# A GpSimd queue in which each product waits for the end of the one before, and value pooling moved to VectorE

## The chip, the core and the metric

The kernel runs on one core of a Trainium2 chip. It uses the core's engines side by side, each with a queue of its own: TensorE (PE; its weight loads are shown apart as PEld), VectorE (DVE), ScalarE (ACT), GpSimd (POOL) and SyncE (SP), which issues the transfers from and to HBM. Engines wait for each other by semaphores. The metric is the time of one execution on the device in microseconds; the median of several runs counts.

## The reference

Three blocks follow one another, all in float32, on 4 batches x 576 positions = 2304 rows of width 512 (8 heads of 64).

```python
# attention; q, k, v are [4, 8, 576, 64]
q_d, k_d, v_d = (x.reshape(B, H, 144, 4, 64).mean(axis=3) for x in (q, k, v))
out_d = sm_attn(q_d, k_d, v_d)                  # attention over 144 pooled positions
out_up = np.repeat(out_d, 4, axis=2)
mask = np.abs(pos[:, None] - pos[None, :]) < 4  # local attention: 3 keys to either side
scores = np.where(mask, scale * q @ k.T, -1e9)
out_local = softmax(scores) @ v
x = out_up + out_local                          # then heads joined: [2304, 512]
# block 1: h = x @ w_in [512, 2048]
g = np.maximum(h, 0) + alpha * np.minimum(h, 0)
x = g @ w_out                                   # [2048, 512]
# block 2
xn = x / np.sqrt(np.mean(x * x, -1, keepdims=True) + 1e-6) * rms_g
g, val = xn @ w_gate, xn @ w_val                # [512, 1536] each
out = (g * sigmoid(g) * val) @ w_out2           # [1536, 512]
```

## The kernel before

**Matmuls.** Each float32 operand is split in two half-precision parts (`split` at L435 to L437: ACT writes the high part, L436, DVE the low part, L437), and a product is three matmuls. Block 1 works on blocks of 384 columns (two groups of 192): `h_mm` (matmuls at L1429, ACT's relu at L1433, DVE's correction at L1435, then `split`) makes the hidden layer, `o_mm` (L1446) the output. Block 2 works on pairs of such blocks with fewer, larger products (`pair_f`, L1681).

**Attention.** Batch 0 and the first group of batch 1 use matmuls for the local attention too (`Dense`). The other eight groups, 4 to 11, use `local_tasks`: 128 partitions hold 32 stretches of rows x 4 pairs of heads, 6 rows each. For two rows and one head of the pair at a time, one POOL operation multiplies q by its seven neighbouring keys (L542; the product has 2 x 7 x 64 = 896 elements per partition and is named `prod`), and DVE sums over the 64 (L553). After the softmax (POOL at L566 to L584, small), one POOL operation multiplies the seven weights by the values (L596, `prod` again), and DVE sums over the seven (L609). That is 6 products of either kind per group, 48 and 48 in all, through two `prod` buffers.

**Pooling.** `down_tasks` does the pooled attention of batches 1 to 3, one pair of heads at a time (4 per batch). For each of q, k and v it loads a tile `sd` (72 partitions x 2 x 2 x 256), ACT squares v for a bound on its size (L691), and `pool` sums four rows to one by two additions: in place into `sd` (L705, 512 elements), then into `qkp` for q and k or `dd` for v (L707, 256 elements). In batch 1 DVE does them, in batches 2 and 3 POOL. The next head's load of v goes into the buffer that these sums read.

**Weights.** Between the other work, weights are decoded from int32 halves (L1183, L1186 on ACT, L1188 on DVE, 768 elements, two inputs in SBUF) and split.

**The order.** All instructions are traced first; `issue_order` (L76) then plays the program through with a cost for each instruction (`cost`), lags between engines, and a port that DVE and POOL share in its model, and orders each engine's queue by the due times that come out. A table `LEADS` shifts the due times of ranges of instructions, in ns, before the last pass. The order is then written down as dependencies between neighbours in a queue, without any semaphore wait:

```python
    info = mybir.DependencyInfo(mybir.DependencyClass.NoSync, mybir.DependencyReason.DATA)
    for q in best[1].values():
        for a, b in zip(q, q[1:]):
            tc.add_manual_dep(insts[b], insts[a].name, info, reason="issue order")
```

So a POOL instruction waits by semaphore only for what it needs: its inputs, and its buffer. Each engine takes its queue strictly in this order.

Of the kernel before, what the change touches and what calls it, by code (L numbers as in the profile page):

```python
# [18 lines left out]
def view(ap, dims, off=0, parts=None):  # L19
# [2 lines left out]


LEADS = (
# [48 lines left out]
)  # L73


def issue_order(tc, nc, groups, rounds=40):  # L76
# [3 lines left out]
    count = range(len(insts))  # L80
# [21 lines left out]
    def psum(a):  # L102
        return "PSUM" in str(a.tensor.space)
# [34 lines left out]
    def cost(k, ins, outs):  # L138
        i, e = insts[k], eng[k]
        if not outs:  # L140
            return 60.0
        o, n = outs[0], free(outs[0])
        if e == "SP":
            return transfer(o, ins[0])[0]
        if e == "PE":
            if wide(ins[0]) == 2:
                return max(25.0, n / 2.4 + 2.5)
            return n * 2 / 2.4 + 3 if i.is_transpose else n * 4 / 2.4 + (128 if n < 64 else 8)
        n = max([n] + [free(a) for a in ins[:1]])
        extra = len([a for a in ins[1:] if free(a) == 1 and n > 1])  # L150
        if e == "Activation":
            return (61 if psum(ins[0]) else 103) + n / 1.2 + 93 * (extra + len(outs) - 1)
        if e == "DVE":
            if i.opcode == "Reciprocal":
                return 89 + 6.25 * n
            fast = i.opcode in ("TensorScalarPtr", "TensorCopy") and not any(psum(a) for a in ins)
            fast = fast and len([a for a in ins if free(a) > 1]) < 2
            return 89 + n / (1.92 if fast else 0.96) + 60 * (extra > 0)
        if n <= 4 and ins:
            return 1200.0  # L160
        if i.opcode == "TensorTensor":
            return 148 + 100 * (list(o.ap)[-1][0] == 7) + n * (1.667 if any(list(a.ap)[-1][0] == 0 for a in ins) else 2.104)
        return 36 + 0.83 * n if i.opcode == "Memset" else 370 + 6 * n if i.opcode == "ISA" else 200 + 2.0 * n

    aps = [tuple([a.bass_ap for a in l if hasattr(a, "bass_ap")] for l in (i.ins, i.outs)) for i in insts]
# [4 lines left out]
    def second(k, ins):  # L170
# [5 lines left out]
        if n > 1:  # L176
            return True
        return insts[k].opcode in ("TensorScalarPtr", "TensorCopy") and not any(psum(a) for a in aps[k][0] + aps[k][1])

    shared = [second(k, aps[k][0]) for k in count]  # L180
    users = {}
# [19 lines left out]
    for k, (ins, outs) in enumerate(aps):  # L201
        for l, wr in ((ins, False), (outs, True)):
            for a in l:
                n = a.tensor.name
# [55 lines left out]
    def run(P, S, prio, fwd, d):  # L260
# [9 lines left out]
        for _ in count:  # L270
# [11 lines left out]
                real[k] += max(0.0, port - t)  # L282
                port = t + real[k]
            end[k] = t + real[k]
            clock[e] = end[k] if held[k] is None else t + held[k]
            seq[e].append(k)
            for s in S[k]:
                left[s] -= 1
# [18 lines left out]
            lead[k] += by  # L307
    end, seq, d = run(preds, succs, lead, True, dur)
    best = max(end), seq, lead
    info = mybir.DependencyInfo(mybir.DependencyClass.NoSync, mybir.DependencyReason.DATA)  # L310
    for q in best[1].values():
        for a, b in zip(q, q[1:]):
            tc.add_manual_dep(insts[b], insts[a].name, info, reason="issue order")


@with_exitstack
def kernel(
# [14 lines left out]
    nc = tc.nc  # L332
# [339 lines left out]
    def down_tasks(b, h, tags=(None, None, None), solo=False, dd=("prod", "prod")):  # L672
# [21 lines left out]
        def pool(nm):  # L694
            def f():
# [5 lines left out]
                        st["qkp"] = pool_of(tq).tile([SH, 2, 2, 2, D], F32, tag=tq, name="qkp")  # L701
                    p = st["qkp"][:, 0 if nm == "q" else 1]
                t = t.rearrange("p a j r -> p (a j) r")
                eng = nc.gpsimd if b > 1 and nm in "qkv" else nc.vector
                eng.tensor_tensor(out=t[:, :, 0:2 * D], in0=t[:, :, 0:2 * D], in1=t[:, :, 2 * D:4 * D],  # L705
                                        op=ALU.add)
                eng.tensor_tensor(out=p.rearrange("p a j d -> p (a j) d"), in0=t[:, :, 0:D],  # L707
# [1421 lines left out]
```

## Time and profile before

| | us |
|---|---|
| median of 3 runs | 921.95 |
| lowest, highest | 921.83, 924.78 |
| the profiled execution | 923.82 |
| its span, first to last instruction | 922.1 |
| PE busy | 884.4 |
| DVE busy | 722.5 |
| ACT busy | 567.5 |
| POOL busy | 408.6 |

The profile is of one execution. Its own time is 1.72 us longer than the span that the trace covers, and 1.87 us above the median. Busy times overlap, since the engines work side by side: the one to look at is the engine whose gaps the others fill or make.

### The profile page before, as it was taken

The numbers are of one execution on the slowest core, as the hardware profiler recorded it, in microseconds if no ns is written. First come the engines' busy times: TensorE is split into PE (matmuls) and PEld (weight loads), VectorE is DVE, ScalarE is ACT, GpSimd is POOL, SyncE is SP. The second block draws the span as 40 slices with busy tenths as digits, with TensorE's granted clock in tenths as the row PEclk, the third lists the DMA queues.
The fourth block names the chain that finished last, engine by engine and source line by source line (L and its number), as shares of the span: only waits on it lengthen the run. The fifth ranks groups of instructions, "written<-read, shape, count | busy, mean of one in ns | idle before, by whom it ended". The sixth has DMA issues, their size and how long they took to land.

```text
span 922.1 us, 16731 instructions
## 1 busy us (share of the span) xinstructions
PE 884.4 (96%) x6394; PEld 591.0 (64%) x6394; DVE 722.5 (78%) x1342; ACT 567.5 (62%) x1332; POOL 408.6 (44%) x330
## 2 busy tenths in 40 slices
PE   6977999999999999899999999999999999999997
PEld 5766877689856666566666666654466654566686
DVE  4789987798756887897889898999888883177872
ACT  4999985443674347774598688984266742256730
POOL 1100105887999899687310344211415100077730
PEclk9997999999999999999999999999999999999999
DMA  9976351263423104440152102220100001100001
GB/s 218 296 277 201 93 177 40 61 202 109 122 75 110 48 26 102 140 133 1 36 168 72 36 1 70 86 87 24 35 12 1 1 1 36 33 1 1 1 18 52
DMA packets 54110, 73.80 MB, mean 80 GB/s; under 512 B 22202, under 2 KB 35918, under 8 KB 54030
## 3 DMA queue, kind: packets, MB, share of 16 engines
q1 hardware_dynamic: 54030, 72.74, 27.0%
q8 instruction: 50, 0.82, 0.4%
q14 instruction: 30, 0.25, 0.1%
HBM read 68.01 MB, written 4.72 MB: 79 GB/s over the span
## 4 chain that ended last, share of the span: by engine, by line
PE 76%; DVE 8%; ACT 6%; POOL 3%; issue 3%; DMA 3%; SPq 1%; DVEq 0%; POOLq 0%; ACTq 0%
PE hps L1429 16%; PE acc L1446 15%; PE pa L1681 14%; PE oacc L1804 10%; PE pf L1681 7%; PE pb L1681 3%; PE px L1924 3%; PE py L1924 1%; PE lsps L953 1%; POOL prod L542 1%; DVE xt L437 1%; POOL prod L596 1%; DMA sd<-in_v_dram 1%; DVE ls L553 1%; ACT wr L1183 1%
## 5 line engine op out<-in xcount | busy, mean ns | idle before, releaser
L1429 PE MATMUL hps<-xt,wi 128*128 128x192 f16 (+1 forms) x1536 | 328.7, 290 | 13.9 <-DVE g L437 8.9
L1446 PE MATMUL acc<-ghl,wo 128*128 128x384 f16 (+1 forms) x960 | 228.2, 311 | 2.2 <-ACT ghl L436 2.2
L1429 PEld LDWEIGHTS <-wi 128*128 128x128 f16 x1536 | 150.2, 101 | 61.4 <-issue 10.0
L1446 PEld LDWEIGHTS <-wo 128*128 128x128 f16 x1344 | 128.9, 98 | 64.3 <-issue 9.0
L1681 PEld LDWEIGHTS <-ws 128*128 128x128 f16 x864 | 84.9, 99 | 57.1 <-issue 1.5
L542 POOL TENSOR_TENSOR prod<-cq,ckv 128x896 f32<-128x896 f32 x48 | 101.8, 2135 | 36.2 <-PE tps L1064 28.2
L1804 PE MATMUL oacc<-wi,wo 128*128 128x512 f16 x360 | 99.4, 379 | 0.0
L1681 PEld LDWEIGHTS <-w 128*128 128x128 f16 x648 | 63.8, 99 | 41.9 <-issue 0.6
L1433 ACT ACTIVATE g<-hps 128x384 f32<-128x384 f32 x96 | 47.0, 489 | 68.5 <-PE hps L1429 68.1
L1435 DVE SCALAR_TENSOR_TENSOR hps<-g,oma,hps 128x192 f32<-128x192 f32 (+1 forms) x128 | 66.2, 518 | 28.1 <-ACT g L1433 27.5
L596 POOL TENSOR_TENSOR prod<-ls,ckv 128x896 f32<-128x896 f32 x48 | 86.2, 1847 | 3.5 <-DVE lo L609 2.8
L1446 PE MATMUL acc<-g,wo 128*128 128x384 f16 (+1 forms) x384 | 73.0, 286 | 0.1
L1681 PE MATMUL pb<-x,w 128*128 128x384 f16 x216 | 67.7, 326 | 0.0
L1681 PE MATMUL pa<-x,w 128*128 128x384 f16 x216 | 66.3, 326 | 0.0
L1661 POOL TENSOR_TENSOR ws<-w 128x768 f32<-128x768 f16 x12 | 22.7, 1899 | 97.4 <-DVE ws L1568 41.5
L1804 PEld LDWEIGHTS <-wo 128*128 128x128 f16 x360 | 35.2, 98 | 40.1
L1689 DVE TENSOR_TENSOR sn<-pf,sn 128x384 f32<-128x384 f32 x45 | 24.9, 553 | 43.7 <-PE pf L1681 38.8
L436 ACT ACTIVATE ghl<-hps,grp 128x384 f16<-128x384 f32 (+1 forms) x73 | 42.0, 576 | 26.2 <-DVE hps L1435 15.8
L1686 ACT ACTIVATE sn<-pa 128x384 f32<-128x384 f32 x66 | 31.7, 486 | 42.6 <-PE pa L1681 42.1
L609 DVE TENSOR_REDUCE lo<-prod 128x128 f32<-128x896 f32 x48 | 51.8, 1079 | 7.7 <-POOL prod L596 7.5
L1873 POOL TENSOR_TENSOR wr<-wi 128x512 f32<-128x512 f16 x12 | 15.7, 1305 | 87.7 <-DMA out_dram<-ob 79.6
L553 DVE TENSOR_REDUCE ls<-prod 128x14 f32<-128x896 f32 x48 | 51.7, 1079 | 2.8 <-POOL prod L542 2.7
(366 smaller groups left out, 2117.9 us busy)
## 6 DMA issues: line engine op xcount, KB each, us to landing
wr<-in_moe_w_out_dram SPq DMA_DIRECT2D x18, 512.0 KB
wr<-in_moe_w_in_dram SPq DMA_DIRECT2D x10, 768.0 KB
wr<-in_moe_w_gate_dram SPq DMA_DIRECT2D x8, 768.0 KB
wr<-in_moe_w_val_dram SPq DMA_DIRECT2D x8, 768.0 KB
ckv<-in_k_dram SPq DMA_DIRECT2D x7, 768.0 KB
ckv<-in_v_dram SPq DMA_DIRECT2D x7, 768.0 KB
wr<-in_moe_w_out_dram SPq DMA_DIRECT2D x20, 256.0 KB
out_dram<-ob SPq DMA_DIRECT2D x14, 256.0 KB
```

Source lines behind the costliest of these rows:

```text
L436: nc.scalar.activation(out=hi, in_=src, func=AF.Copy, scale=s)
L542: engs[i].tensor_tensor(out=pr, in0=view(st["q"][:, j, t:t + TP], [[D, TP], [0, ND], [1, D]]), in1=view(st["k"][:, j, t:t + TP], [[D, TP], ...
L553: nc.vector.tensor_reduce(out=st["s"][:, j, t:t + TP], in_=st.pop(("p", i)), axis=AX.X, op=ALU.add)
L596: engs[i].tensor_tensor(out=over(pr, i), in0=view(st["s"][:, j, t:t + TP], [[ND, TP], [1, ND], [0, D]]), in1=view(st["v"][:, j, t:t + TP], ...
L609: nc.vector.tensor_reduce(out=st["o"][:, t:t + TP, j], in_=view(pr, [[ND * D, TP], [ND, D], [1, ND]]), axis=AX.X, op=ALU.add)
L1429: nc.tensor.matmul(ps[:, j], wi[:, f + j, a, kk * 128:(kk + 1) * 128], x[:, b_, kk, c0:c0 + n], start=(i == 0), stop=(i == 3 * KK - 1))
L1433: nc.scalar.activation(out=g, in_=ps, func=AF.Relu, scale=-1.0)
L1435: nc.vector.scalar_tensor_tensor(out=ps[:, j], in0=g[:, j], scalar=oma[:, f + j:f + j + 1], in1=ps[:, j], op0=ALU.mult, op1=ALU.add)
L1446: nc.tensor.matmul(acc[e], wo_f(f)[:, a, e * 128:(e + 1) * 128], hl[:, b_], start=(f == f0 and i == 0), stop=(f == f1 and i == 2))
L1681: nc.tensor.matmul(ps, w[:, a, kk, c:c + 128], x[:, b_, kk], start=(start and n == 0), stop=(n == 3 * K2 - 1), skip_group_check=True)
L1804: nc.tensor.matmul(acc, uhl(f)[:, h, a, tt * 128:(tt + 1) * 128], w[:, b_, f % 3], start=(f == fs[0] and i == 0), stop=(f == fs[-1] and i ...
L1924: nc.tensor.matmul(ps, two(u[g])[:, a, tt * 128:(tt + 1) * 128], w(g, b_), start=(start and g == 0 and i == 0), stop=(g == F2 - 1 and i == 2),
```

## The change

Four things change. (1) In the order written down at the end, the POOL instruction behind one that writes `prod`, `sd`, `qkp` or `dd` now gets a dependency with a semaphore wait: it starts only when that one has ended. The model of `issue_order` puts 120 ns between the two. (2) In batches 2 and 3, `pool("v")` runs on DVE; q and k stay on POOL. (3) The model's costs change for POOL's two-input operations (without a repeated operand 124 + 2.203 n ns instead of 148 + 2.104 n; the 100 ns for a stride of 7 no longer apply to the products with v, whose weights are repeated) and for DVE operations that write with a stride of 8 (65 + 1.8 n; the additions at L645). (4) `LEADS` is another table. No instruction is added or dropped, and no transfer.

```diff
@@ LEADS = (
-    (8123, 8158, -2000), (927, 928, 1000), (8102, 8103, 7000), (8208, 8396, -1500), (2202, 2286, 4000),
...
-    (6529, 6694, 2500), (696, 697, -22500), (8777, 8780, 1500), (6999, 7000, -8000),
+    (8102, 8103, 7000), (776, 777, -500), (3486, 3544, 1500), (7335, 7386, 500), (5591, 5593, -500),
...
+    (6319, 6321, 14500),
 )
@@ def cost(k, ins, outs):
                 return 89 + 6.25 * n
+            if list(o.ap)[-1][0] == 8:
+                return 65 + 1.8 * n
...
         if i.opcode == "TensorTensor":
-            return 148 + 100 * (list(o.ap)[-1][0] == 7) + n * (1.667 if any(list(a.ap)[-1][0] == 0 for a in ins) else 2.104)
+            if any(list(a.ap)[-1][0] == 0 for a in ins):
+                return 148 + n * 1.667
+            return 124 + 100 * (list(o.ap)[-1][0] == 7) + n * 2.203
@@ def issue_order
+    apart = [120.0 if eng[k] == "Pool" and aps[k][1] and
+             aps[k][1][0].tensor.name.split("_")[0] in ("prod", "sd", "qkp", "dd") else 0.0 for k in count]
...
-            clock[e] = end[k] if held[k] is None else t + held[k]
+            clock[e] = end[k] + apart[k] if held[k] is None else t + held[k]
...
-    info = mybir.DependencyInfo(mybir.DependencyClass.NoSync, mybir.DependencyReason.DATA)
+    info, wait = [mybir.DependencyInfo(c, mybir.DependencyReason.DATA)
+                  for c in (mybir.DependencyClass.NoSync, mybir.DependencyClass.Sync)]
     for q in best[1].values():
         for a, b in zip(q, q[1:]):
-            tc.add_manual_dep(insts[b], insts[a].name, info, reason="issue order")
+            tc.add_manual_dep(insts[b], insts[a].name, wait if apart[a] else info, reason="issue order")
@@ def down_tasks, pool(nm)
-                eng = nc.gpsimd if b > 1 and nm in "qkv" else nc.vector
+                eng = nc.gpsimd if nm in {2: "qk", 3: "qk"}.get(b, "") else nc.vector
```

## Rows read from the trace of the kernel before

**Rows 1.** The page: busy time of PE, and shares of the last chain

```profile
PE 884.4 (96%) x6394; PEld 591.0 (64%) x6394; DVE 722.5 (78%) x1342; ACT 567.5 (62%) x1332; POOL 408.6 (44%) x330
...
PE 76%; DVE 8%; ACT 6%; POOL 3%; issue 3%; DMA 3%; SPq 1%; DVEq 0%; POOLq 0%; ACTq 0%
```

**Rows 2.** PE's waits, 147 to 435 us: total, times, longest

```profile
PE hps L1429 <- DVE g L437: 2.4, 3, 1.8
PE acc L1446 <- ACT ghl L436: 2.2, 1, 2.2
PE atps L758 <- ACT dd L749: 2.0, 2, 1.5
PE ltps L997 <- POOL dls L983: 1.5, 1, 1.5
PE hps L1429 <- DVE ghl L437: 1.3, 1, 1.3
PE hps L1429 <- DVE xt L437: 1.2, 1, 1.2
```

**Rows 3.** Stretches: length, busy of PE, PEld, DVE, ACT, POOL; clock, DMA

```profile
240.00:280.00 40.00, 37.76 (x314) 26.52 (x312) 24.91 (x42) 25.05 (x83) 36.58 (x30) 0.96 0.36 102
260.00:380.00 120.00, 120.00 (x819) 75.72 (x818) 91.59 (x148) 62.91 (x184) 109.08 (x79) 1.00 0.28 81
```

**Rows 4.** Timeline of DVE: start, duration, operation, idle time before

```profile
177.78 2.73 DVE L979 TENSOR_SCALAR dlsum<-dlsum 96x8 f32<-96x8 f32 x1 [0.61 <-ACT dls L973]
...
190.82 4.02 DVE L437 SCALAR_TENSOR_TENSOR xt<-dls,sc,xt 128x192 f16<-128x192 f32 x1
...
203.12 0.40 DVE L437 SCALAR_TENSOR_TENSOR xt<-dls,sc,xt 128x192 f16<-128x192 f32 x1
...
374.82 3.93 DVE L1188 SCALAR_TENSOR_TENSOR wc<-wr 128x768 int32<-128x768 int32 x1 [1.02 <-ACT wr L1186]
...
382.94 2.67 DVE L1188 SCALAR_TENSOR_TENSOR wc<-wr 128x768 int32<-128x768 int32 x1 [0.27 <-ACT wr L1186]
...
388.96 0.96 DVE L1188 SCALAR_TENSOR_TENSOR wc<-wr 128x768 int32<-128x768 int32 x1
...
395.25 2.42 DVE L1188 SCALAR_TENSOR_TENSOR wc<-wr 128x768 int32<-128x768 int32 x1
...
848.93 1.36 DVE L1867 SCALAR_TENSOR_TENSOR w<-th,w 128x384 f16<-128x384 f32 x1
```

**Rows 5.** Timeline of POOL, same columns

```profile
177.42 1.29 POOL L705 TENSOR_TENSOR sd<-sd 72x512 f32<-72x512 f32 x1
178.65 1.84 POOL L596 TENSOR_TENSOR prod<-ls,ckv 128x896 f32<-128x896 f32 x1
...
189.03 2.13 POOL L542 TENSOR_TENSOR prod<-cq,ckv 128x896 f32<-128x896 f32 x1
...
193.90 0.72 POOL L707 TENSOR_TENSOR qkp<-sd 72x256 f32<-72x256 f32 x1
...
211.98 5.22 POOL L596 TENSOR_TENSOR prod<-ls,ckv 128x896 f32<-128x896 f32 x3
...
373.02 2.14 POOL L542 TENSOR_TENSOR prod<-cq,ckv 128x896 f32<-128x896 f32 x1
...
414.06 10.54 POOL L542 TENSOR_TENSOR prod<-cq,ckv 128x896 f32<-128x896 f32 x5
...
848.64 1.24 POOL L1893 TENSOR_TENSOR wo<-th,wo 128x384 f32<-128x384 f32 x1
849.96 1.21 POOL L1895 TENSOR_TENSOR sn<-th,wo 128x384 f32<-128x384 f32 x1
```

**Rows 6.** Groups of DVE by shape: first pooling sum, batch 1

```profile
L705 DVE TENSOR_TENSOR sd<-sd 72x512 f32<-72x512 f32 x12 | 8.2, 680 | 2.3 <-DMA sd<-in_q_dram 1.8 <-DMA sd<-in_k_dram 0.5
```

**Rows 7.** The chain that ended last, near 245 us: start, duration

```profile
243.04 0.79 POOL dd L707
...
245.09 8.75 DMA sd<-in_v_dram
```

87 rows, old and new, of the table LEADS are left out of this document.

## The prediction

> **What bounds the kernel now.** I read the page first: TensorE (PE) is busy for 884.4 of 922.1 us, and the chain that ended last runs over PE for 76%, over VectorE (DVE) for 8%, over GpSimd (POOL) for 3% [rows 1]. So PE's own work sets the time, and a change off PE can only give or take PE's gaps: 922.1 - 884.4 = 37.7 us in all. Next I asked who PE waits for in the stretch in which POOL computes the attention products, 147 to 435 us [rows 2]. The reader is to see six kinds of wait, 2.4 + 2.2 + 2.0 + 1.5 + 1.3 + 1.2 = 10.6 us; most name DVE, or an engine that itself stood behind DVE. Then the table by stretch [rows 3]: from 260 to 380 us PE has no gap (120.00 of 120) although POOL is 91% busy and DVE 76%; from 240 to 280 us the granted clock falls to a mean of 0.96, 1.00 being the upper level of 2.4 GHz. Last I laid the timelines of DVE and POOL side by side [rows 4, 5], and there the cause of the waits is seen.
>
> **What the timelines show.** The DVE operation at 203.12 (192 elements, two inputs in SBUF) takes 0.40 us; the same operation at 190.82 takes 4.02 [rows 4]. POOL meanwhile runs without a break from 189.03 to 193.90 + 0.72 = 194.62, four operations, each starting before the one ahead has ended in the record, and DVE's operation ends at 194.84, just behind the last of them [rows 5]. A correction of a few numbers at 177.78 takes 2.73 us and ends at 180.51: it sat through the rest of the pooling sum at 177.42 and all of the product at 178.65 (end 180.49). So DVE and POOL exclude each other, and where POOL's next operation is already queued, DVE isn't let in at the end of the present one. The late part of the kernel shows the other case: POOL's operation at 849.96 reads what the one at 848.64 wrote, so it waits; it starts 0.08 us after that one's end (848.64 + 1.24 = 849.88). DVE's operation of 848.93 ends at 850.29, inside the second one: the pause of 0.08 us was enough [rows 4, 5].
>
> **The waits, gain.** The change puts such a pause behind each product and pooling sum. I go through the PE waits with a DVE operation held over more than one POOL operation ahead of them.
> - 177.78: let in at 177.42 + 1.29 = 178.71 instead of 180.49, 1.8 us sooner. PE's wait for the probabilities (1.5, row "ltps") shrinks, but POOL must first finish the product of 178.65, now started about 0.2 us later: 1.15 us saved.
> - 190.82: let in at 189.03 + 2.13 = 191.16, done near 191.5 instead of 194.84, 3.3 us sooner. The longest wait of "hps <- DVE g" (1.8) goes: 1.8.
> - 374.82: took 3.93 us, where the same form at 388.96 takes 0.96, so it came in only near 378.75 - 0.96 = 377.8. Let in at the end of the product that it met, 373.02 + 2.14 = 375.16, it is some 2.6 us sooner; the wait "atps" (longest 1.5) goes: 1.5.
> - 395.25: 2.42 us, over one end between two products: 1.2 of "hps <- DVE xt".
>
> Together 1.15 + 1.8 + 1.5 + 1.2 = 5.65 us. The operation at 382.94 (2.67) was held by one product only; the pause doesn't help it, and the 1.3 us behind it stay.
>
> **The waits, price.** Five products q x k end to end take 10.54 us, so they start (10.54 - 2.13) / 4 = 2.10 apart; with a pause it is 2.13 + 0.08 = 2.21, 0.11 more. Products with v: (5.22 - 1.84) / 2 = 1.69 apart, then 1.84 + 0.08 = 1.92: 0.23 more. A pooling sum: 1.23 (177.42 to 178.65), then 1.29 + 0.08 = 1.37, 0.14 more. At most 48 x 0.11 + 48 x 0.23 + 32 x 0.14 = 20.8 us on POOL; less, to nothing, where the next operation waits for something else anyway. Against it POOL loses the v sums of two batches (8 pairs of heads): 8 x (1.23 + 0.72) = 15.6 us. So POOL's stage grows by at most 5.2 us. PE waits for POOL directly only once in the stretch (the 1.5 above) [rows 2], and from 260 to 380 us POOL has 120 - 109.1 = 10.9 us of idle time [rows 3]; I take 0 for it. If that cover is gone, the 5.2 us come on top.
>
> **The v sums on DVE.** Eight pairs of heads, two operations each, by DVE's own row for the other batch 0.68 and, for the second one of half the size, at most as much [rows 6]: at most 10.9 us more on DVE, whose idle time from 260 to 380 us alone is 120 - 91.6 = 28.4 us. Both have two SBUF inputs, so each now stands in front of POOL's operations: held up to one product, 2.13 us, while POOL is 91% busy, so some 14.5 of 16 are held. Queued behind them on DVE are the corrections and splits of the hidden layer, for which PE waits. What one hold costs PE isn't shown for these operations; the nearest rows bound it: from 260 to 380 us PE had no gap at all beside full queues (below: 0), and the operation of 382.94, held by one product, has 1.3 us behind it (above). As that one is longer (0.96 of its own, with another long hold just ahead of it at 374.82), I put the upper bound at half, 0.65: 14.5 x 0.65 = 9.4. I take 0.2 apiece, 2.9 us, nearer to the row without a gap, because most of these sums fall into its stretch.
>
> Moving them also moves a transfer. The load of the next pair's v into the same buffer was issued at 245.09, after POOL's v sum of 243.04 let the buffer go; it lands 8.75 us later, and ScalarE, stuck on that v, kept back what PE needed [rows 7]: the wait "acc <- ACT ghl" of 2.2. Behind that gap the clock dropped to its lower level (1.2 instead of 2.4 GHz): (1 - 0.96) x 40 = 1.6 us more. If DVE does that sum sooner, up to 3.8 us go; if it does it as late, none. No new DMA is issued, SP's queue only waits for another engine. I take half, 1.9.
>
> **The table of shifts** reorders every queue. It has no price in any row. Outside this stretch it can gain or lose; I take 0, and 2 us to either side for the range.
>
> **Sum.** 5.65 + 1.9 - 2.9 = 4.65 us. The profiled execution took 923.82 us (922.1 of span, 1.7 around it), so 919.2 by its own time; the median of the three runs stands 1.87 below it: 921.95 - 4.65 = 917.3, rounded to 917.
>
> **A rule weighed.** The row at 190.82 kept DVE out over three ends of POOL operations. The Trainium skill, "SBUF — State Buffer", section "Who interferes with whom", says that the port pair that both share is locked for one whole instruction and the other side is blocked until it finishes. By that alone DVE would have come in at 191.16 without any new wait, and the change would buy nothing there; the measured 194.84 speaks against it.
>
> **Rivals.**
> 1. *The forecast*: DVE comes in at each product's end, part of it paid back by the v sums. 912.5 (5.65 + 3.8, nothing paid) to 919. Chance 0.64.
> 2. *DVE takes over the waiting (slower).* The v sums on DVE are held in front of POOL's products and in turn hold the hidden layer's corrections. Price up to 9.4 us, with POOL's 5.2 on top when its lag reaches PE: 14.6 - 5.65 = 9 us slower at worst. It decides from about 0.6 us per hold (14.5 x 0.6 = 8.7, above 5.65 + 2.8 of what can be told): then about 926. For it: the 1.3 behind 382.94. Against it: no gap of PE from 260 to 380 us. Chance 0.13.
> 3. *The pause doesn't open the way*, because in the 0.08 us the port isn't given up behind these operations: the gaps stay, the waits cost POOL at most 5.2, mostly covered, the load of v gives 0 to 3.8. About 921. For it: the two operations of 848.64 and 849.96 are of other shapes than the products. Against it: DVE did come in there. The lock rule above ends in the same place. Chance 0.08.
> 4. *The order gives it back*: the gaps named here close, and the new table opens others of the same size, in the weight preparation ahead of 147 us or behind a moved load. About 921. Chance 0.15.
>
> The three runs of before lie 2.95 us apart; 0.3%, 2.8 us, is about what can be told from no change. Faster by more than that: rival 1, 0.64. Within: 3 and 4, 0.23. Slower: 2, 0.13. The range, 912.5 to 922.7, leaves out rival 2 and the best end of the forecast.
>
> **What would show it.** Right: no DVE operation with two SBUF inputs lasts beyond the end of the one POOL operation that it met, between 147 and 435 us, and PE's waits there fall from 10.6 to about 5 us; products start 0.1 to 0.2 us further apart, 0.08 us behind an end; DVE's v sums last 0.4 to 2.8 us. Wrong: DVE held over several products as before (3); PE waiting for DVE behind a v sum (2); the gaps of the first 147 us grown (4); the clock still dipping between 240 and 280 us (the load's half).

## The result, and the profile after

The changed kernel takes 913.39 us (median of 4 runs, 911.58 to 915.09), the kernel before 922.72 beside it (4 runs, 921.83 to 924.78): ratio 0.9896, 95% interval 0.9867 to 0.9924. It is faster, as forecast, by 9.3 us where 4.65 were forecast. Its profiled execution took 912.48 us, of which 910.8 are span, 11.3 less than the span of before. Line numbers stand 3 higher than before (L542 is now L545, L596 is L599, L705 is L708).

The page of after, busy times and the last chain:

```profile
PE 885.3 (97%) x6394; PEld 592.8 (65%) x6394; DVE 729.8 (80%) x1358; ACT 570.0 (63%) x1332; POOL 401.8 (44%) x314
...
PE 85%; ACT 6%; DVE 3%; DMA 2%; POOL 2%; issue 1%; SPq 0%; DVEq 0%; POOLq 0%; ACTq 0%
```

Against [rows 1], PE is as busy as it was, its idle time fell from 37.7 to 910.8 - 885.3 = 25.5 us, and the share of DVE in the chain from 8% to 3%.

PE's waits of after from 147 to 435 us (total, times, longest):

```profile
PE atps L761 <- ACT dd L752: 1.0, 1, 1.0
PE sps L733 <- ACT qkT L723: 0.4, 1, 0.4
PE hps L1432 <- DVE ghl L440: 0.2, 1, 0.2
```

These three lines stand in place of the six of [rows 2]: 1.6 us for 10.6.

The stretches of after (length, busy of PE, PEld, DVE, ACT, POOL; clock, DMA):

```profile
147.00:205.00 58.00, 58.00 (x585) 47.62 (x584) 49.67 (x88) 26.94 (x83) 53.35 (x37) 1.00 0.37 115
205.00:260.00 55.00, 53.45 (x586) 46.63 (x584) 49.14 (x81) 37.00 (x121) 49.14 (x34) 1.00 0.40 122
240.00:280.00 40.00, 39.03 (x303) 26.84 (x301) 35.79 (x60) 23.30 (x72) 36.17 (x23) 1.00 0.37 111
260.00:380.00 120.00, 119.76 (x802) 75.47 (x801) 97.36 (x169) 64.65 (x175) 104.56 (x70) 1.00 0.29 82
380.00:435.00 55.00, 55.00 (x350) 34.46 (x348) 49.49 (x82) 34.01 (x62) 40.94 (x24) 1.00 0.22 64
```

From 147 to 205 and from 380 to 435 us PE has no gap left. From 260 to 380 DVE is 97.4 us busy instead of 91.6 [rows 3], and PE still loses only 0.24. Eight of the sixteen v sums stand between 216 and 257 us; in the stretch from 205 to 260 us, which holds them, PE loses 1.55 us. The mean clock between 240 and 280 us is 1.00.

The timeline of DVE after (start, duration, operation, idle time before):

```profile
185.98 1.14 DVE L982 TENSOR_SCALAR dlsum<-dlsum 96x8 f32<-96x8 f32 x1
...
191.30 1.26 DVE L440 SCALAR_TENSOR_TENSOR xt<-dls,sc,xt 128x192 f16<-128x192 f32 x1
...
216.50 1.88 DVE L708 TENSOR_TENSOR sd<-sd 72x512 f32<-72x512 f32 x1 [0.16 <-ACT dd L694]
...
240.93 2.24 DVE L708 TENSOR_TENSOR sd<-sd 72x512 f32<-72x512 f32 x1 [0.50 <-ACT dd L694]
243.20 1.81 DVE L710 TENSOR_TENSOR dd<-sd 72x256 f32<-72x256 f32 x1
```

and that of POOL, same columns:

```profile
178.32 8.78 POOL L545 TENSOR_TENSOR prod<-cq,ckv 128x896 f32<-128x896 f32 x4
...
190.22 2.13 POOL L545 TENSOR_TENSOR prod<-cq,ckv 128x896 f32<-128x896 f32 x1
192.42 0.86 POOL L986 TENSOR_TENSOR dls<-dls,dlsum 96x408 f32<-96x408 f32 x1
...
215.69 4.69 POOL L545 TENSOR_TENSOR prod<-cq,ckv 128x896 f32<-128x896 f32 x2
```

The four products of 178.32 end at 187.10, and the correction of 185.98, which met the last of them, ends at 187.12 (at 177.78 before it lasted 2.73 us [rows 4]). The split of 191.30 meets the product that ends at 192.35 and ends at 192.56; its twin of before sat through four operations of POOL for 4.02 us. Behind the product of 190.22 the next operation starts at 192.42, 0.07 after that end; over the whole trace 88 of the 96 products are followed within 0.06 to 0.11 us of their end, and none is overlapped by its successor. The four products start (8.78 - 2.13) / 3 = 2.22 apart, as worked out (2.21).

The v sums on DVE, groups by shape from 147 to 435 us (busy, mean ns of one, idle before):

```profile
L708 DVE TENSOR_TENSOR sd<-sd 72x512 f32<-72x512 f32 x8 | 10.7, 1341 | 2.7 <-ACT dd L694 2.7
L710 DVE TENSOR_TENSOR dd<-sd 72x256 f32<-72x256 f32 x8 | 7.3, 912 | 0.0
```

The first takes 1341 ns where the undisturbed one took 680 [rows 6], the second 912 where DVE's own ones of batches 0 and 1 took 415 in the trace of before. So they are held by 8 x 0.66 + 8 x 0.50 = 9.3 us in all, none of them past the end of more than one POOL operation. The longest takes 2.24 us; the forecast gave them 0.4 to 2.8.

They aren't free. The largest gap that PE has left in the stretch, 1.0 us ahead of a matmul into `atps`, stands behind the two held sums of 240.93 and 243.20. The chain that ended last runs through them:

```profile
240.93 2.25 DVE sd L708
...
244.94 0.41 DVE hps L1438
245.46 0.42 ACT dd L752
245.92 0.26 PE atps L761
```

The run with waits behind the products only, below, has the same order and no such gap; there the first sum of that pair took its own 0.69 us. In the three other runs of this order, where that sum took 2.07 to 2.16 us, the same matmul waits 1.0 us.

### The profile page after: what moved, and what is told of

It reads as the page before. It is cut to its first block, busy times and chain, and to the rows that moved or that the text cites. A ratio compares the mean times of both kernels' runs of the same rounds, so it can differ in the third digit from the quotient of the medians.

```text
span 910.8 us, 16778 instructions
## 1 busy us (share of the span) xinstructions
PE 885.3 (97%) x6394; PEld 592.8 (65%) x6394; DVE 729.8 (80%) x1358; ACT 570.0 (63%) x1332; POOL 401.8 (44%) x314
## 4 chain that ended last, share of the span: by engine, by line
PE 85%; ACT 6%; DVE 3%; DMA 2%; POOL 2%; issue 1%; SPq 0%; DVEq 0%; POOLq 0%; ACTq 0%
PE hps L1432 18%; PE acc L1449 17%; PE pa L1684 14%; PE oacc L1807 10%; PE pf L1684 7%; PE pb L1684 3%; PE px L1927 3%; POOL prod L599 1%; PE py L1927 1%; PE lsps L956 1%; PE tps L868 1%; ACT wr L1186 1%; PE lops L1012 1%; ACT wi L439 1%; PE ltps L1000 1%
## 5 line engine op out<-in xcount | busy, mean ns | idle before, releaser
L1449 PE MATMUL acc<-ghl,wo 128*128 128x384 f16 (+1 forms) x960 | 231.0, 310 | 0.0
L545 POOL TENSOR_TENSOR prod<-cq,ckv 128x896 f32<-128x896 f32 x48 | 105.5, 2197 | 41.4 <-DVE hps L1438 35.3
L599 POOL TENSOR_TENSOR prod<-ls,ckv 128x896 f32<-128x896 f32 x48 | 91.3, 1903 | 9.8 <-DVE lo L612 6.5
L1807 PE MATMUL oacc<-wi,wo 128*128 128x512 f16 x360 | 95.4, 379 | 0.2 <-ACT ob L1811 0.2
L1449 PE MATMUL acc<-g,wo 128*128 128x384 f16 (+1 forms) x384 | 70.3, 286 | 0.1
```

Source lines behind the costliest of these rows:

```text
L545: engs[i].tensor_tensor(out=pr, in0=view(st["q"][:, j, t:t + TP], [[D, TP], [0, ND], [1, D]]), in1=view(st["k"][:, j, t:t + TP], [[D, TP], ...
L599: engs[i].tensor_tensor(out=over(pr, i), in0=view(st["s"][:, j, t:t + TP], [[ND, TP], [1, ND], [0, D]]), in1=view(st["v"][:, j, t:t + TP], ...
L1449: nc.tensor.matmul(acc[e], wo_f(f)[:, a, e * 128:(e + 1) * 128], hl[:, b_], start=(f == f0 and i == 0), stop=(f == f1 and i == 2))
L1807: nc.tensor.matmul(acc, uhl(f)[:, h, a, tt * 128:(tt + 1) * 128], w[:, b_, f % 3], start=(f == fs[0] and i == 0), stop=(f == fs[-1] and i ...
```

## Experiments

Each ratio is to the kernel before on the same chip; times of different groups come from different chips, so compare the ratios. Three groups: one half of the change at a time under the orders at hand, all four combinations without a table, and the waits divided by kind.

**The waits alone.** The kernel before with its own order on every queue; only the waits are added.

```diff
...
-            tc.add_manual_dep(insts[b], insts[a].name, info, reason="issue order")
+            tc.add_manual_dep(insts[b], insts[a].name, wait if apart[a] else info, reason="issue order")
```

> The kernel before, every queue in its old order, with the semaphore wait behind each prod, sd, qkp and dd and nothing else. The port theory (VectorE comes in at each product's end): VectorE's long holds of 2.4 to 4.0 us shrink to at most one product, PE's waits at 181, 194, 382 and 397 us go, about 5.6 us minus what the pauses cost GpSimd: 916 to 919 beside a before of 922.7 (ratio 0.993 to 0.996). The theory that order and table made the gain: the waits only slow GpSimd, ratio 1.000 to 1.005. The theory that the moved v sums (their load) made it: 1.000.

Measured: 920.78 us, ratio 0.9979 (0.9966 to 0.9993), 0.2% faster. That is less than the port theory's 0.993 to 0.996, and no loss as the theory of order and table had it. The gaps that the prediction listed did close, but others came in their place. PE's two largest waits by total, 147 to 435 us:

```profile
PE hps L1432 <- DVE ghl L440: 1.7, 6, 0.5
PE acc L1449 <- ACT ghl L439: 1.5, 1, 1.5
```

The gap behind the late load of v stays (1.5 for 2.2 [rows 2]), and of the six small waits for the hidden layer's splits five stand ahead of matmuls for which PE didn't wait before.

**The new order without waits.** The changed kernel, its order planned with the pauses; the waits are left out.

```diff
-            tc.add_manual_dep(insts[b], insts[a].name, wait if apart[a] else info, reason="issue order")
+            tc.add_manual_dep(insts[b], insts[a].name, info, reason="issue order")
```

> The changed kernel, every queue in its own order, without the new waits. The port theory: VectorE is held over several products again, now with the sixteen v sums too: some 6 us or more of the 9.3 us are lost, 919 to 926. The order theory: stays within 2 us of the changed kernel's 913.4. The v sum theory: also 913 to 915.

Measured: 922.51 us, ratio 0.9983 (0.9967 to 0.9999). So in the new order the waits are worth 0.87% (0.9983 to 0.9896), 8 us, as the port theory expected (919 to 926). DVE's timeline, one line:

```profile
220.17 4.58 DVE L708 TENSOR_TENSOR sd<-sd 72x512 f32<-72x512 f32 x1 [0.23 <-ACT dd L694]
```

and POOL's beside it:

```profile
218.07 4.23 POOL L545 TENSOR_TENSOR prod<-cq,ckv 128x896 f32<-128x896 f32 x2
222.27 0.71 POOL L710 TENSOR_TENSOR qkp<-sd 72x256 f32<-72x256 f32 x1
222.95 1.25 POOL L708 TENSOR_TENSOR sd<-sd 72x512 f32<-72x512 f32 x1
224.28 1.05 POOL L710 TENSOR_TENSOR qkp<-sd 72x256 f32<-72x256 f32 x1
```

One v sum starts at the end of the first product of 218.07, sits through the second and through the two sums behind it (222.27 and 222.95), and gets in only near 224.20, when the last of these ends; the fifth operation then lasts 1.05 us where its twin of 222.27 takes 0.71. PE's two largest waits there, 147 to 435 us:

```profile
PE hps L1432 <- DVE ghl L440: 4.1, 3, 1.6
PE sps L733 <- DVE xt L440: 1.8, 1, 1.8
```

The gap "acc <- ACT ghl" isn't among PE's waits, although there are no pauses: it went with the new order and the v sums on DVE, which this run doesn't tell apart.

**The v sums alone, under a fitted table.** Two kernels change only the engine of the v sums and keep the table of the kernel that they come from; the planner then makes another order, for which that table wasn't made. The first is the changed kernel with all sums of batches 2 and 3 on POOL:

```diff
-                eng = nc.gpsimd if nm in {2: "qk", 3: "qk"}.get(b, "") else nc.vector
+                eng = nc.gpsimd if b > 1 else nc.vector
```

> The changed kernel with the v sums back on GpSimd; waits, costs and table kept, the order is made anew and the table no longer fits it exactly. The port theory: most of the gain stays, 914 to 918. The v sum theory: the gap and the clock dip near 254 us come back, 3.8 us or more, 917 to 920. The order theory: the table misfits, anything from 915 to 922.

The second is the kernel before with the v sums of batches 2 and 3 on DVE, without waits:

```diff
-                eng = nc.gpsimd if b > 1 and nm in "qkv" else nc.vector
+                eng = nc.gpsimd if b > 1 and nm in "qk" else nc.vector
```

> The kernel before with only the v sums of batches 2 and 3 on VectorE, old costs and table, no waits. The port theory: the sixteen v sums are held over several products each, 922 to 930. The v sum theory: the load near 245 us comes sooner, 917 to 919. The order theory: the old table misfits, 922 to 926.

Measured: 934.49 (1.0109, 1.0089 to 1.0129) and 972.2 (1.0517, 1.0488 to 1.0545). Both lie outside every range that was expected of them, and neither says what the sums cost by themselves: ahead of 147 us PE idles 20.8 and 25.2 us, after 435 us (to the end) 14.8 and 20.8, where the kernel before has 20.5 and 6.6. What the second does show is how bad the holds can become; its v sums, by shape, 147 to 435 us:

```profile
L707 DVE TENSOR_TENSOR dd<-sd 72x256 f32<-72x256 f32 x8 | 16.0, 2005 | 0.0
L705 DVE TENSOR_TENSOR sd<-sd 72x512 f32<-72x512 f32 x8 | 15.2, 1902 | 3.6 <-ACT dd L691 3.6
```

**Waits and v sums without any table.** To take the table out of the question, four kernels have an empty one and the same planner's costs, so that each gets the planner's plain order; the pause is in the planner where the waits are in the kernel.

```diff
-LEADS = (
-...
-)
+LEADS = ()
...
-    apart = [120.0 if eng[k] == "Pool" and aps[k][1] and
+    apart = [0.0 if eng[k] == "Pool" and aps[k][1] and
```

(the second edit, with the plain dependency of the order without waits above, is in two of the four; two have the v sums' line of before.)

> One of four kernels with an empty table of shifts and the changed kernel's costs: with and without the waits (in the queue and in the model alike), v sums on VectorE or GpSimd. This one has both parts of the change. The port theory: it beats the same without waits by 5 us or more, and beats v on GpSimd with waits by 0 to 4. The table theory (the 9 us come from a table that fits): all four lie within some 4 us of each other, and 10 us or more above the changed kernel.

> Empty table, no waits, v sums on VectorE. The port theory: the slowest of the four, since sixteen more two-input operations are held over several products. The table theory: as the other three.

> Empty table, waits, v sums on GpSimd. The port theory: faster than the same without waits by some 4 us, and 0 to 4 us slower than with v on VectorE (the load near 245 us). The table theory: as the other three.

> Empty table, no waits, v sums on GpSimd: the kernel before but for costs and table. Against the 922.7 us of before it shows what a table is worth at all. The port theory and the table theory both expect it slower than before, by 5 to 20 us.

| empty table | no waits | waits | the waits are worth |
|---|---|---|---|
| v sums on POOL | 936.89 (1.0132, 1.0094 to 1.0171) | 927.40 (1.0039, 1.0022 to 1.0056) | 9.5 us |
| v sums on DVE | 941.75 (1.0190, 1.0126 to 1.0255) | 919.21 (0.9957, 0.9938 to 0.9977) | 22.5 us |
| moving them costs | 4.9 us | -8.2 us | |

The four times lie up to 22.5 us apart, not within 4, so the theory that the table alone made the gain falls. The port theory had the order of the four right, but expected some 4 us of the waits with the sums on POOL (9.5) and at most 4 of the move with waits (8.2).

What the v sums' move brings hangs on the waits. With them it gains 8.2 us, clear of the intervals. Without them it is 4.9 us slower, but there the two intervals overlap, so a loss isn't shown. Nor are the 8.2 us the sums' own: of them 3.2 are gaps of PE between 147 and 435 us (4.6 against 1.4), the rest lies in other stretches and in PE's own busy time, since the planner orders the two kernels differently throughout. The sums' rows, by shape, 147 to 435 us, with DVE doing them and no waits:

```profile
L664 DVE TENSOR_TENSOR sd<-sd 72x512 f32<-72x512 f32 x8 | 14.3, 1793 | 0.1
L666 DVE TENSOR_TENSOR dd<-sd 72x256 f32<-72x256 f32 x8 | 13.9, 1739 | 0.0
```

and with the waits:

```profile
L664 DVE TENSOR_TENSOR sd<-sd 72x512 f32<-72x512 f32 x8 | 11.0, 1377 | 2.7 <-ACT dd L650 2.7
L666 DVE TENSOR_TENSOR dd<-sd 72x256 f32<-72x256 f32 x8 | 7.8, 977 | 0.0
```

With waits and the sums on POOL, ScalarE stands behind the late load of v, as in the kernel before; its wait there,

```profile
ACT dd L650 <- DMA sd<-in_v_dram: 3.4, 2, 3.2
```

is 0.4 us, once, with the sums on DVE:

```profile
ACT dd L650 <- DMA sd<-in_v_dram: 0.4, 1, 0.4
```

The kernel with waits, v sums on DVE and no table at all beats the kernel before with its table.

**Which waits.** The changed kernel, same order, with waits behind the 96 products only; behind the 32 pooling sums only; and behind every operation of POOL.

```diff
-... wait if apart[a] else info, reason="issue order")
+... wait if apart[a] and aps[a][1][0].tensor.name.startswith("prod") else info, reason="issue order")
```

(the second with "not" ahead of the last test, the third with the condition eng[a] == "Pool".)

> The changed kernel with the same order on every engine, but GpSimd waits for the end only behind the 96 attention products, no longer behind its 32 pooling sums. Theory A (what counts are the ends inside rows of long instructions; of those products follow products far more often than sums follow sums, and the products are the long ones): almost all of the 8 us that separate the changed kernel from the same order without waits stays, ratio to before 0.989 to 0.992, 913 to 915.5 us. Theory B (it is the total of pauses, each end alike): 96 of 128 of the 8 us stay, 915.5, ratio 0.992 or more. Theory C (the ends behind sums decide, since VectorE's own v sums and corrections stand there): over 918, ratio above 0.995.

> The other half: the changed kernel with the same order, waits only behind GpSimd's 32 pooling sums, none behind products. Theory A: VectorE is held over two to six products again, 920 to 922, ratio 0.996 to 0.999, close to the order without any wait. Theory B: a quarter of the 8 us comes back, 920. Theory C: most of it comes back, below 917, ratio below 0.994.

> The changed kernel with the same order, and a wait behind every one of GpSimd's instructions (masks, corrections and reductions too), not only behind products and pooling sums. Theory A (long rows of products decide): nothing more to win, 912 to 915, ratio 0.988 to 0.991, within 0.15% of the changed kernel. Rival: the short operations between products also keep VectorE out and the remaining 2 to 3 us of gaps between 205 and 380 us close: 910 to 911.5, ratio below 0.988. Other rival: some 150 more pauses of 0.1 to 0.2 us make GpSimd late for TensorE: 916 or more.

Measured: 915.85 us, 0.9893 (0.9870 to 0.9915); 922.52, 0.9974 (0.9958 to 0.9990); 917.06, 0.9912 (0.9891 to 0.9933). Theory A holds by the ratios: with the waits behind the products alone the changed kernel's 0.9896 is reached. Those behind the sums bring 0.09% over none (0.9983), which isn't clear of the intervals, and more waits win nothing. The last, 0.9912, stands at the upper edge of what Theory A gave it; the 0.0016 between it and the changed kernel lies within the intervals, so a small price of the further pauses isn't ruled out.

The kernel with waits behind products only has one line of PE's waits from 380 to 440 us, where the changed kernel, with the same order, has none:

```profile
PE hps L1432 <- DVE ghl L440: 2.3, 2, 1.6
```

DVE's timeline ahead of it:

```profile
399.35 2.91 DVE L1191 SCALAR_TENSOR_TENSOR wc<-wr 128x768 int32<-128x768 int32 x1
402.18 0.61 DVE L1438 SCALAR_TENSOR_TENSOR hps<-g,oma,hps 128x384 f32<-128x384 f32 x1
402.70 0.61 DVE L440 SCALAR_TENSOR_TENSOR ghl<-hps,grp,ghl 128x384 f16<-128x384 f32 x1
...
406.85 2.71 DVE L1191 SCALAR_TENSOR_TENSOR wc<-wr 128x768 int32<-128x768 int32 x1
```

and POOL's:

```profile
392.63 8.81 POOL L545 TENSOR_TENSOR prod<-cq,ckv 128x896 f32<-128x896 f32 x4 [0.86 <-DVE lo L612]
401.52 1.48 POOL L1399 TENSOR_TENSOR ry<-ry,mhalf 128x3 f32<-128x3 f32 x1
```

The weight operation of 399.35 starts just behind the start of the last of the four products (one of 2.15 us that ends at 401.44), sits through the whole of it, and two operations that PE needs stand behind it: 1.6 us. This is the hold by one product that the pauses don't open, as at 382.94 before [rows 4]; the run with waits everywhere has it too (2.4 us, twice, longest 1.6). The same two weight operations in the changed kernel's profile:

```profile
398.21 0.95 DVE L1191 SCALAR_TENSOR_TENSOR wc<-wr 128x768 int32<-128x768 int32 x1
...
403.75 1.30 DVE L1191 SCALAR_TENSOR_TENSOR wc<-wr 128x768 int32<-128x768 int32 x1
```

and the four products beside them:

```profile
391.65 9.51 POOL L545 TENSOR_TENSOR prod<-cq,ckv 128x896 f32<-128x896 f32 x4 [0.87 <-DVE lo L612]
```

There the first of the two came in at the end of the third product and took its own 0.95 us; now the fourth product is held instead, and the four take 9.51 us where they took 8.81. The second met only the tail of a product. So in these profiles some 2 us hang on the tenths of a microsecond by which a DVE operation meets or misses the pause. The medians don't show them (0.9893 against 0.9896): other executions may meet it or not.

## Why the prediction was right in direction and half in size

PE's idle time by stretch, from the windows of one profiled execution each (length minus busy, us):

| kernel | 0 to 147 | 147 to 435 |
|---|---|---|
| before | 20.5 | 10.6 |
| waits alone | 21.8 | 6.8 |
| new order, no waits | 17.9 | 9.7 |
| new order, waits behind sums | 18.0 | 8.0 |
| new order, waits behind products | 18.8 | 2.9 |
| new order, waits everywhere | 17.4 | 4.6 |
| after | 16.1 | 1.8 |

From before to after the profiled span is 11.3 us shorter: PE's gaps fell by 4.4 us ahead of 147 us and by 8.8 between 147 and 435, grew by 1.0 behind, and PE itself was busy 0.9 longer. The sum had forecast 4.65 us, all of it in the middle stretch, and nothing for the rest. PE's busy time differs from run to run (883.1 to 886.9 us in these seven), so the gaps alone don't give a kernel's time.

- **The mechanism of the waits** is shown: with the pause DVE comes in at the end of the product that it met, without it DVE's operations sit through as many as four operations of POOL. The rule that was weighed against the trace (the Trainium skill, "SBUF — State Buffer", "Who interferes with whom": the lock lasts one instruction) describes the kernels with waits; in those without, one operation is held through three, which the rule by itself doesn't give. Rival 3 falls.
- **Their gain (5.65)** was of the right kind, but isn't one number. In the old order the four gaps that it listed close (5.9 us, matmul by matmul), but others open elsewhere: in all 3.8 us of gaps go (10.6 to 6.8), and the time falls by 0.21%, 1.9 us; in the new one 8.0 (9.7 to 1.8) and 0.87%; without a table 9.5 or 22.5 us. The prediction counted the gaps that close and none that open.
- **Their price on POOL (0)** held: spacing 2.22 as worked out, POOL's busy time 401.8 for 408.6, and no wait of PE for POOL in the stretch.
- **The v sums on DVE (-2.9)** is the step that failed, in its size. The holds came as foreseen (9.3 us in sixteen sums), but 0.2 us of PE's time for each held sum was too much: one pair costs PE the 1.0 us shown above, from 260 to 380 us, where the other eight stand, PE lost 0.24 us, and of PE's waits that name DVE 0.2 us are left in the whole stretch. Rival 2 falls with it. It may describe a kernel without waits, where moving the sums was 4.9 us slower, but that isn't clear of the noise.
- **The moved load (+1.9 of 3.8)** came in full as to its gap. ScalarE's wait for that v is one line of after, 147 to 435 us:

```profile
ACT dd L694 <- DMA sd<-in_v_dram: 0.4, 1, 0.4
```

where the trace of before has

```profile
ACT dd L691 <- DMA sd<-in_v_dram: 3.0, 1, 3.0
```

The gap (2.2) is gone in the new order without waits too, and stays with the waits alone (1.5); moved sums and new order weren't parted here. The dip of the clock is gone in after, but with the waits alone too, in spite of that gap, so it isn't the load's by itself.
- **The table (0, 2 either way)** was put too low ahead of 147 us. The five kernels with the new order have 16.1 to 18.8 us of gaps there, mean 17.6; the two with the old one 20.5 and 21.8: some 3.5 us. That is the new order as a whole, table, costs and moved sums together, and not all of it reaches the time: without waits the new order gains 1.6 us. The clock's dips there differ from run to run, and part of it may be arrival of transfers; why the new order does better there wasn't tried. Rival 4 falls.

So the direction was right by its mechanism; that the time came close to the best end of rival 1 (912.5) is partly luck, since 4.4 us came from a stretch that the sum had at nothing.

What the sum missed is that its terms aren't independent. Of the 1.04%, waits alone give 0.21 and the new order alone 0.17; the other 0.66%, 6.1 us, appear only with both. Why they do is argued, not shown. The table of before is worth some 12 us over the plain order (ratio 1.0132 without it, with the new costs) on a chip where DVE is held over several operations: it hides part of the damage that the waits remove, and the waits shift everything behind them. An order made with the pause in its costs meets what POOL then does. In favour: with the sums on POOL the waits bring 1.9 us in the old order and 9.5 without a table. The other reading is that the waits are worth more because the new order has sixteen more operations on DVE to let in: without a table they bring 22.5 us with the sums on DVE and 9.5 with them on POOL. Both can hold at once; how well either order fits wasn't measured by itself.

## What to carry to other kernels

Where two engines exclude each other, look at whether the one with the long operations has the next one already queued: a wait behind its long operations (0.08 us each here) lets the other engine in, and here it was enough behind the products, the longest ones. Price such an edit together with what else is planned on both engines, since moving work onto the excluded engine gained 8.2 us with the waits and nothing without them (4.9 us slower, within the noise). A schedule that was fitted by hand or by search may carry the old stalls in it: measure a new mechanism with the schedule made anew, or without one, before judging it small (here 0.2% in the old order, 1.0% in the new one with all else that changed).

## What the hardware showed unasked

- Exclusion over many operations: 4.58 us for a sum that takes 0.68 alone, through three operations of POOL, one of them only 0.71 us long. Between queued operations there is hardly a break: of the 96 products of before, 78 are followed by an operation that starts before their end in the record, of after none.
- The pause cuts both ways. In after the four products of 391.65 take 9.51 us, because a DVE operation of 0.95 us came in behind the third of them. And the one operation of 3 columns behind the held weight operation above took 1.48 us, and in after, where no DVE operation was in its way, 0.89:

```profile
401.24 0.89 POOL L1399 TENSOR_TENSOR ry<-ry,mhalf 128x3 f32<-128x3 f32 x1
```

So where DVE is in first, POOL's record grows: the exclusion is mutual.
